# Probabilities copied by DMA and transposed as fp32r, and six held units for the mixing step

## The chip, the cores and the metric

The kernel runs on one core of one Trainium2 chip. The metric is the time of one execution on the device, in microseconds. A core has TensorE (PE, with its weight loads listed apart as PEld), VectorE (DVE), ScalarE (ACT), GpSimd (POOL) and SyncE (SP), which here only issues DMAs.

## The reference

Two layers: attention with a decay over 8 batches x 8 heads, 576 tokens, head size 64, and then a mixing layer over 512 channels.

```python
scores = q @ k.T / 8 + cum[:, None] - cum[None, :]   # cum = cumsum(log(clip(f)))
attn = softmax(where(causal, -1e9, scores))
x = concat_heads(attn @ v)                     # (8, 576, 512)
u = x + (x.transpose(0, 2, 1) @ U @ V).transpose(0, 2, 1)   # rank 32, over the tokens
out = u + maximum(u @ w_ch1, 0) @ w_ch2        # 512 -> 2048 -> 512
```

All of it is in fp32.

## The kernel before, in words

**Numbers in two parts.** Where precision is needed, an fp32 value is held as a high part rounded to fp32r and a low part, and a product is three fp32r matmuls (high by high, low by high, high by low). The first `NF = 6` pairs of heads use plain fp32 matmuls instead.

**Pairs and steps.** The attention works on pairs of heads: 4 pairs a batch, 32 in all (`p`). `step(t)` has ten slots (`s`), and handles three pairs at once: pair `p` is scored, the pair one step behind (`a`) has its probabilities transposed, and the one two steps behind (`c`) is multiplied with the values and normalised. For each of the two heads (`j`) and each of four blocks of 128 queries (`i`) `score` makes a tile of up to 512 columns; in slots 0 to 3 those of head 0, in slots 6 to 9 those of head 1 (two of them in 7 to 9 follow a first one at the end of 6). `score_tail` does the last 64 queries of both heads, in slots 4 and 5.

**What follows a score.** `defer(phase, fn, slots)` puts work off to a later slot, where it runs by phase. One slot after a score DVE adds the mask and takes the row extremum (L364), and ACT makes the exponential (L372, the tail at L400) into a tile of pool `sb2`, tag `P{i}`, or `Ptl`. In the next step `turn_p` transposes these tiles on PE, 128 x 128 at a time, against an identity (L444: 20 a pair), `turn_tail` the tail (L461: 4) and `turn_small` its last 64 columns (L479: 1). ACT copies each result from PSUM as the high part (L419), DVE subtracts for the low part (L422). `values` multiplies with the values (L568 to L574); for the result the halves of a PSUM tile are added crosswise, through a tile `cr` that ACT copies (L583) and DVE adds (L579). `turn_x` brings the result back, and it is scaled into `xn[b % 3]`.

**Mixing and feed-forward.** After the fourth pair of a batch follow ten mixing units, one a slot in the steps of `MIX`: five products with U and V (`hmix`, L656), four transposes of u (`tu`, L670) and that of the tail (`tv`, L679). Their PSUM tiles come from `psF`, which has two banks. The six of 16 blocks of the hidden layer that lie in the sweep are `ffn_units`: `l1` (L719, 12 matmuls a unit) and `l2` (L737, 6 matmuls a unit, three units to one `psF` tile). They fill PE between the attention's work (`run_filler`): by a credit in the slots of `ROOM`, and in the mixing step from the `HELD = 4` last units of the batch before, in slots 0, 1, 3 and 5. The sums of an `l2` tile and of x go through a tile `ost` to DRAM (`accd`), u goes to DRAM as `ud`; after the sweep the other ten blocks are computed from these.

**Order.** PE's order is the program's throughout, SP's too from step 8 on; a DMA issue that waits holds up all that follow on SP. The order on the other engines is set by the planner of the framework.

In the listing that follows the line numbers are those of the profile.

Of the kernel before, what the change touches and what calls it, by code (L numbers as in the profile page):

```python
# [18 lines left out]
DM = H * D  # L19
# [22 lines left out]
def tile_decay_attention_moe(ctx, tc, qk, v, f, U, V, w1, w2, out):  # L42
# [41 lines left out]
    sf2 = pool("sf2", 2)  # L84
# [6 lines left out]
    sb3 = pool("sb3", 3)  # L91
    psF = ctx.enter_context(tc.tile_pool(name="psF", bufs=2, space=PSUM))
# [28 lines left out]
    ident = cst.tile([P, P], F32, name="ident")  # L121
    make_identity(nc, ident)
# [16 lines left out]
    def decay_log():  # L139
        fr = sb.tile([B * H, S], F32, tag="xT", name="fr")  # L140
        fl = sb.tile([B * H, S], F32, tag="cr", name="fl")
        cm = sb.tile([B * H, 4, S], F32R, tag="PT", name="cm")
        return fr, fl, cm
# [46 lines left out]

    def load_w(u):
# [4 lines left out]
        if kind == "w2":  # L196

            spare = xn[NX - 1].rearrange("p c d -> p (c d)").bitcast(I32)
            if fc % 2:
                raw, a = spare[:, 1536:2560], sb.tile([P, 512], I32, tag="w2a", name=f"stg{u}")  # L200
            else:
                raw, a = spare[:, 0:1024], spare[:, 1024:1536]
# [142 lines left out]

    scored = [0]
# [8 lines left out]
    def score(p, j, i):  # L355
# [25 lines left out]
    def score_tail(p, x):  # L381
# [14 lines left out]
        def use():  # L396
            if x == 1:
                z["ptl"] = sb.tile([P, S], F32, tag="Ptl", name=f"Ptl{p}")
                for y in range(2):
                    nc.scalar.activation(  # L400
                        z["ptl"][:, hw * y : hw * y + hw], z["tl"][y][:, :hw], AF.Exp, bias=z["nm"][:, 9:10],
                        scale=-1.0, accum_out=z["sm"][:, 8 + y : 9 + y],
                    )

# [21 lines left out]
    def turn_p(p, j, g):  # L426
# [16 lines left out]
        for x, (c, i) in enumerate(grp):  # L443
            nc.tensor.transpose(tp[:, P * x : P * x + P], z["P"][j][i][:, P * c : P * c + P], ident)  # L444
# [12 lines left out]
    def turn_tail(p):  # L457
        z = st[p]
        tp = z["tv"][:, 512:1024]
        for c in range(NM):  # L460
            nc.tensor.transpose(tp[:, P * c : P * c + P], z["ptl"][:, P * c : P * c + P], ident)  # L461
# [13 lines left out]
    def turn_small(pa, px):  # L475

        tq = psT.tile([P, 512], F32, tag="T", name=f"Ty{pa}_{px}")
        if pa is not None:
            nc.tensor.transpose(tq[0:64, 0:P], st[pa]["ptl"][:, MAIN:S], ident)  # L479
# [75 lines left out]
    def values(p, j):  # L555
# [4 lines left out]
        if j == 0:  # L560
            z["xT"] = sb.tile([P, S], F32, tag="xT", name=f"xT{p}")
            z["cr"] = sb.tile([P, S], F32, tag="cr", name=f"cr{p}")
        VS, xT, cr = z["VS"], z["xT"], z["cr"]
# [13 lines left out]

        def total():
            nc.vector.tensor_tensor(xT[OWN[j]], pv[OWN[j], X0 : X0 + S], cr[OTH[j]], op=ALU.add)  # L579
# [3 lines left out]
        defer(1, lambda: nc.scalar.copy(cr[OTH[j]], pv[OTH[j], X0 : X0 + S]))  # L583
# [59 lines left out]
    def mix_units(b):  # L643
# [30 lines left out]
        def tv():  # L674
# [9 lines left out]
            def use():  # L684
                for x, t in enumerate((uh, ul)):
                    if b < B - 1:
                        nc.sync.dma_start(ud[b, :, x], t.bitcast(F32)[:, :, 0:MAIN])
                    if b % 2:
                        jt = b // 2
                        nc.sync.dma_start(ud[B, :, x, :, P * jt : P * jt + P], t.bitcast(F32)[:, :, MAIN : MAIN + P])  # L690

            defer(4, use, 2)
# [8 lines left out]
    def ffn_units(b):  # L701
# [3 lines left out]
        for t0, nt in groups:  # L705
# [24 lines left out]
            def l2(x, part, t0=t0, g=g):  # L730
# [14 lines left out]
                def use():  # L745
                    if b == B - 1 and ci < NM:
                        nc.vector.tensor_tensor(X[:, ci], ps, X[:, ci], op=ALU.add)
                        return
                    ost = sf2.tile([P, DM], F32, tag="ost", name=f"ost{b}_{ci}")
                    if ci < NM:  # L750
                        nc.vector.tensor_tensor(ost, ps, X[:, ci], op=ALU.add)  # L751
                        nc.sync.dma_start(accd[b, ci], ost)
                    else:
                        nc.vector.tensor_tensor(ost[0:64], ps[0:64], X[0:64, NM], op=ALU.add)
                        nc.vector.tensor_tensor(ost[64:128], ps[64:128], xn[(b - 1) % NX][0:64, NM], op=ALU.add)
                        nc.sync.dma_start(accd[B, b // 2], ost)

                defer(1, use)

# [9 lines left out]
    HELD = 4  # L769
# [485 lines left out]
```

## Time and profile before

| | |
|---|---|
| median of 3 runs | 1265.49 us (1256.07, 1265.49, 1266.22) |
| the profiled execution | 1256.17 us, its span 1254.3 us |
| PE busy | 1210.9 us, 97% of the span |
| PE weight loads | 1074.2 us, 86% |
| DVE, ACT, POOL busy | 893.8, 645.2, 325.2 us |
| DMA | 125.89 MB, mean 100 GB/s |

PE rows are matmuls, PEld rows weight loads. Matmuls are pipelined, so the sum of their durations is more than the time they take; the distance from one start to the next is what one of them costs. The attention sweep ends at about 700 us, the feed-forward work that was filled into it a little later, and what remains is the rest of the hidden layer.

### The profile page before, as it was taken

To read this page: it belongs to the slowest core of one execution; us is meant where nothing else is said; L and a number is where in the kernel's file an instruction comes from. 1 tells how busy PE (TensorE), PEld (TensorE's weight loads), DVE (VectorE), ACT (ScalarE), POOL (GpSimd) and SP (SyncE) were. 2 spreads that over 40 slices of the span, in tenths; PEclk is the share of its full clock that TensorE was granted. 3 is DMA by queue.
4 is the path that set the end of the run, shared out by engine and by line. 5 is a ranking of instruction groups with operands and counts; after the bars stand their busy time and mean duration, and the time that the engine had idled before them with its cause. 6 is when DMAs were issued, how large, how long until landed. Compare 5 with 4: busy or idle time off the path is not lost.

```text
span 1254.3 us, 21662 instructions
## 1 busy us (share of the span) xinstructions
PE 1210.9 (97%) x7686; PEld 1074.2 (86%) x7686; DVE 893.8 (71%) x2306; ACT 645.2 (51%) x1723; POOL 325.2 (26%) x310
## 2 busy tenths in 40 slices
PE   5999999999999999999999989999999999999998
PEld 3776888998898998988989878888988888888887
DVE  6767588778878768778777699976565565655553
ACT  5666787867777767768667343332122221212221
POOL 4353555434454443545442000000000000000000
PEclk9999999999999999999999999999999999999999
DMA  7435232532435325235413256121221303213010
GB/s 193 120 103 157 66 106 80 172 96 76 141 94 157 110 72 168 75 83 163 110 57 104 79 173 258 53 68 40 96 101 34 135 18 118 84 52 134 1 34 34
DMA packets 67547, 125.89 MB, mean 100 GB/s; under 512 B 7360, under 2 KB 31936, under 8 KB 65392
## 3 DMA queue, kind: packets, MB, share of 16 engines
q1 hardware_dynamic: 67312, 124.50, 32.3%
q8 instruction: 61, 1.00, 0.3%
q14 instruction: 46, 0.38, 0.1%
q10 hardware_dynamic: 128, 0.01, 0.0%
HBM read 88.68 MB, written 35.78 MB: 99 GB/s over the span
## 4 chain that ended last, share of the span: by engine, by line
PE 84%; DVE 9%; ACT 4%; issue 2%; DMA 1%; POOL 0%; SPq 0%; ACTq 0%; DVEq 0%; POOLq 0%
PE O L1004 20%; PE M L1097 16%; PE A L719 10%; PE B L737 9%; PE V L568 5%; PE T L444 4%; PE S L343 3%; PE S L340 2%; PE Hb L990 2%; PE S L344 2%; PE V L525 2%; PE Tt L628 1%; PE Tu L670 1%; PE St L340 1%; ACT G L303 1%
## 5 line engine op out<-in xcount | busy, mean ns | idle before, releaser
L1117 DVE TENSOR_TENSOR sum<-M,sum 128x256 f32<-128x256 f32 x280 | 114.6, 422 | 161.1 <-PE M L1097 159.8
L981 ACT ACTIVATE bh<-sum 128x256 fp32r<-128x256 f32 x160 | 66.7, 418 | 257.9 <-DVE sum L1117 257.9
L372 ACT ACTIVATE P<-S,nm 128x128 f32<-128x128 f32 (+3 forms) x256 | 136.2, 532 | 66.2 <-DVE nm L364 61.8
L364 DVE CUSTOM_DVE_ANT_0 S<-S,mask 128x128 f32<-128x128 f32 (+3 forms) x256 | 125.9, 495 | 59.9 <-PE S L344 39.0
L1004 PE MATMUL O<-b2h,bh 128*128 128x512 f32 x360 | 142.7, 396 | 0.0
L1004 PE MATMUL O<-b2l,bh 128*128 128x512 f32 x360 | 142.2, 395 | 0.0
L1004 PE MATMUL O<-b2h,bl 128*128 128x512 f32 x360 | 141.6, 393 | 0.0
L719 PE MATMUL A<-uh,w1h 128*128 128x256 f32 (+1 forms) x384 | 120.6, 314 | 1.7 <-DVE hl L723 1.7
L719 PE MATMUL A<-ul,w1h 128*128 128x256 f32 (+1 forms) x384 | 113.5, 296 | 0.0
L719 PE MATMUL A<-uh,w1l 128*128 128x256 f32 (+1 forms) x384 | 113.5, 295 | 0.0
L303 POOL CAST G<-qk 64x576 fp32r<-64x576 f32 x52 | 34.3, 661 | 255.5 <-PE St L344 150.7
L737 PE MATMUL B<-w2h,hh 128*128 128x512 f32 x216 | 90.2, 418 | 2.0 <-DVE ost L751 1.0
L444 PE MATMUL T<-ident,P 128*128 128x128 f32 x544 | 88.1, 279 | 0.3 <-DVE PT L422 0.3
L737 PE MATMUL B<-w2l,hh 128*128 128x512 f32 x216 | 85.0, 394 | 0.0
L737 PE MATMUL B<-w2h,hl 128*128 128x512 f32 x216 | 84.7, 392 | 0.0
L1004 PEld LDWEIGHTS O<-b2l,bh 128*128 128x128 f32 x360 | 67.6, 188 | 16.4
L422 DVE TENSOR_TENSOR PT<-T,PT 128x512 fp32r<-128x512 f32 (+1 forms) x156 | 79.0, 528 | 2.4 <-ACT PT L419 0.8
L568 PE MATMUL V<-PT,VS 128*128 128x448 f32 (+2 forms) x416 | 79.7, 334 | 0.0
L319 POOL TENSOR_TENSOR G<-qk,G 64x576 fp32r<-64x576 f32 x52 | 74.4, 1432 | 16.7 <-ACT G L303 15.5
L1004 PEld LDWEIGHTS O<-b2h,bl 128*128 128x128 f32 x360 | 67.9, 189 | 11.2
L343 PE MATMUL S<-G 128*128 128x128 f32 x208 | 71.9, 350 | 5.6 <-ACT P L372 2.9
L1004 PEld LDWEIGHTS O<-b2h,bh 128*128 128x128 f32 x360 | 67.9, 189 | 10.6
(224 smaller groups left out, 3423.9 us busy)
## 6 DMA issues: line engine op xcount, KB each, us to landing
qk<-in_qk_dram SPq DMA_DIRECT2D x104, 288.0 KB
u<-ud SPq DMA_DIRECT2D x16, 1024.0 KB
sr<-in_w_dram SPq DMA_DIRECT2D x20, 512.0 KB
vr<-in_v_dram SPq DMA_DIRECT2D x32, 256.0 KB
accd<-ost SPq DMA_DIRECT2D x32, 256.0 KB
xn<-accd SPq DMA_DIRECT2D x8, 1024.0 KB
out_dram<-xn SPq DMA_DIRECT2D x32, 256.0 KB
ud<-uh SPq DMA_DIRECT2D x7, 1024.0 KB
```

Source lines behind the costliest of these rows:

```text
L319: em.tensor_tensor(g[own, 1, cols], q[own], gf[own, 0, cols], op=ALU.subtract)
L343: nc.tensor.matmul(ps, G[j][:, 0, c0 : c0 + P], G[j][:, 2, cols], start=first, stop=False)
L364: nc.vector.tensor_tensor_reduce(ps[:, :w], ps[:, :w], mask[:, 512 - w : 512], scale=-SCALE, scalar=3.0e38, op0=ALU.add, op1=ALU.min, accu ...
L372: nc.scalar.activation(pt, ps[:, :w], AF.Exp, bias=z["nm"][:, col : col + 1], scale=-1.0, accum_out=z["sm"][:, col : col + 1])
L422: defer(2, lambda: nc.vector.tensor_tensor(dstl, src, dsth.bitcast(F32), op=ALU.subtract))
L444: nc.tensor.transpose(tp[:, P * x : P * x + P], z["P"][j][i][:, P * c : P * c + P], ident)
L568: nc.tensor.matmul(pv[:, X0 + lo : X0 + S], VS[:, c, j], pt[:, j, OC[c] + lo - P * c : OC[c] + S - P * c], start=x == 0 and c == 0, stop=F ...
L719: nc.tensor.matmul(ps[:, :nt], wt[:, fc, c], ut[:, c, sl], start=m == 0, stop=m == 3 * NDC - 1)
L737: nc.tensor.matmul(ps, ht[:, fc, P * x : P * x + P], wt[:, fc], start=fc == 0 and m == 0, stop=fc == NA - 1 and m == 2,)
L1004: nc.tensor.matmul(po, ht[:, P * x : P * x + P], wt_[i], start=k == 0 and m == 0, stop=k == NB - 1 and m == 2)
L1097: nc.tensor.matmul(ps, a[x][:, c], b[y][:, c], start=m == 0, stop=m == 5)
L1117: nc.vector.tensor_tensor(dst, ps, other, op=ALU.add)
```

## The change

Four things change.

- From pair six on (`p >= NF`) the exponential is written to a tile of a new pool `sb4` (four buffers, tag `stg`), and a DMA on SP's queue, one slot later, copies it to the tile `P{i}` or `Ptl`, which is now of type fp32r. The DMA sees both sides as fp32 and moves the bits as they are. The transposes of these tiles are made as fp32r, with an fp32r identity. The tile `cr` and one staging tile of the weights come from the same four buffers.
- The sums of the second layer are added into `xn` itself and stored from there two slots later; the two halves of the tails are stored one by one.
- The stores of u to DRAM go in pieces of 128 x 512, one a slot.
- `HELD` is 6 in place of 4, and in the mixing step units run in slots 0, 1, 3, 5, 7 and 8. The load of the decay rows of the next pair's head 0 is issued in slot 6 ahead of that slot's other work, in place of slot 7.

```diff
+    sb4 = pool("sb4", 4)
...
-    ident = cst.tile([P, P], F32, name="ident")
-    make_identity(nc, ident)
+    identr = cst.tile([P, P], F32R, name="ident")
+    ident = identr.bitcast(F32)
+    unit = sb.tile([P, P], F32, tag="xl", name="unit")
+    make_identity(nc, unit)
+    nc.gpsimd.tensor_copy(identr, unit)
...
+    def stage(name):
+        return sb4.tile([P, S], F32, tag="stg", name=name)
...
+    def turn(p, dst, src):
+        if p < NF:
+            nc.tensor.transpose(dst, src, ident)
+        else:
+            nc.tensor.transpose(dst.bitcast(F32R), src, identr)
...
-            pt = sb2.tile([P, w], F32, tag=f"P{i}", name=f"P{p}_{j}{i}")
+            pt = sb2.tile([P, w], F32 if p < NF else F32R, tag=f"P{i}", name=f"P{p}_{j}{i}")
             z["P"][j].append(pt)
+            e = pt if p < NF else stage(f"E{p}_{j}{i}")
             nc.scalar.activation(
-                pt, ps[:, :w], AF.Exp, bias=z["nm"][:, col : col + 1], scale=-1.0, accum_out=z["sm"][:, col : col + 1]
+                e[:, :w], ps[:, :w], AF.Exp, bias=z["nm"][:, col : col + 1], scale=-1.0,
+                accum_out=z["sm"][:, col : col + 1],
             )
+            if p >= NF:
+                defer(6, lambda: nc.sync.dma_start(pt.bitcast(F32), e[:, :w]))
...
+                if p >= NF:
+                    defer(6, lambda: nc.sync.dma_start(z["ptl"].bitcast(F32), e))
...
-            nc.tensor.transpose(tp[:, P * x : P * x + P], z["P"][j][i][:, P * c : P * c + P], ident)
+            turn(p, tp[:, P * x : P * x + P], z["P"][j][i][:, P * c : P * c + P])
...
+        def cross():
+            z["cr"] = stage(f"cr{p}_{j}")
+            nc.scalar.copy(z["cr"][OTH[j]], pv[OTH[j], X0 : X0 + S])
...
-                    if b < B - 1:
-                        nc.sync.dma_start(ud[b, :, x], t.bitcast(F32)[:, :, 0:MAIN])
+            pieces = [(x, c) for x in range(2) for c in range(NDC + 1) if (b < B - 1 if c < NDC else b % 2)]
+            for k, piece in enumerate(pieces):
+                defer(4, lambda piece=piece: store(*piece), 2 + k)
...
+                def store():
+                    if ci >= NM:
+                        for r, src in enumerate((X, xn[(b - 1) % NX])):
+                            nc.sync.dma_start(accd[B, b // 2, 64 * r : 64 * r + 64], src[0:64, NM])
+                    elif b < B - 1:
+                        nc.sync.dma_start(accd[b, ci], X[:, ci])
...
-    HELD = 4
+    HELD = 6
...
+            if s == 6 and NF <= nxt_p < NP:
+                place_decay(p + 1, 0)
...
-            if s == 7 and NF <= nxt_p < NP:
-                place_decay(p + 1, 0)
...
-                if filler and (s in (0, 1, 3, 5) or ending):
-                    run_filler()
+                for _ in range(1 if ending else {0:1,1:1,3:1,5:1,7:1,8:1}.get(s, 0)):
+                    if filler:
+                        run_filler()
```

More of the change, by code (lines that the diff above doesn't have):

```diff
@@ L140, in decay_log @@
         fr = sb.tile([B * H, S], F32, tag="xT", name="fr")
-        fl = sb.tile([B * H, S], F32, tag="cr", name="fl")
+        fl = sb.tile([B * H, S], F32, tag="Ptl", name="fl")
         cm = sb.tile([B * H, 4, S], F32R, tag="PT", name="cm")
@@ L199, in load_w @@
             if fc % 2:
-                raw, a = spare[:, 1536:2560], sb.tile([P, 512], I32, tag="w2a", name=f"stg{u}")
+                raw, a = spare[:, 1536:2560], stage(f"stg{u}").bitcast(I32)[:, 0:512]
             else:
@@ L460, in turn_tail @@
         for c in range(NM):
-            nc.tensor.transpose(tp[:, P * c : P * c + P], z["ptl"][:, P * c : P * c + P], ident)
+            turn(p, tp[:, P * c : P * c + P], z["ptl"][:, P * c : P * c + P])
         if p < NF:
@@ L478, in turn_small @@
         if pa is not None:
-            nc.tensor.transpose(tq[0:64, 0:P], st[pa]["ptl"][:, MAIN:S], ident)
+            turn(pa, tq[0:64, 0:P], st[pa]["ptl"][:, MAIN:S])
         if px is not None:
@@ L745, in use @@
                 def use():
-                    if b == B - 1 and ci < NM:
+                    if ci < NM:
                         nc.vector.tensor_tensor(X[:, ci], ps, X[:, ci], op=ALU.add)
                         return
[L749 to L756, printed above, removed]
+                    for r, src in enumerate((X, xn[(b - 1) % NX])):
+                        rows, own = slice(64 * r, 64 * r + 64), src[0:64, NM]
+                        nc.vector.tensor_tensor(own, ps[rows], own, op=ALU.add)
+                def store():
+                    if ci >= NM:
+                        for r, src in enumerate((X, xn[(b - 1) % NX])):
+                            nc.sync.dma_start(accd[B, b // 2, 64 * r : 64 * r + 64], src[0:64, NM])
+                    elif b < B - 1:
+                        nc.sync.dma_start(accd[b, ci], X[:, ci])
                 defer(1, use)
+                defer(6, store, 2)
             units += [(12 * max(nt / 2400, 0.107), lambda fc=fc, l1=l1: l1(fc)) for fc in range(NA)]
@@ L964, in tile_decay_attention_moe @@
     up = pool("up", 2)
+    up2 = pool("up2")
     hp_ = pool("hp", 4)
@@ L1031, in tile_decay_attention_moe @@
     Tl = sf.tile([P, 4, 2, HT], F32R, tag="ul", name="Tl")
-    tmp = [sf2.tile([P, 2, HT], F32, tag="ost", name=f"sum{x}") for x in range(2)]
+    tmp = [up2.tile([P, 2, HT], F32, name=f"sum{x}") for x in range(2)]
     tmp.append(sf.tile([P, 2, HT], F32, tag="TS", name="sum2"))
```

26 lines of the change are left out of this document (13 added, 13 removed).

## The prediction

> **What bounds the kernel now.** I read the first page for the balance of the engines, then the busy times of one window in the middle of the sweep, then the chain of waits in that window.
>
> ```profile
> span 1254.3 us, 21662 instructions
> PE 1210.9 (97%) x7686; PEld 1074.2 (86%) x7686; DVE 893.8 (71%) x2306; ACT 645.2 (51%) x1723; POOL 325.2 (26%) x310
> ...
> PEclk9999999999999999999999999999999999999999
> ...
> 200.00:700.00 500.00, 489.50 (x3329) 445.30 (x3328) 392.67 (x1107) 363.14 (x1019) 226.35 (x198) 1.00 0.39 111
> ...
> by line: PE A L719 20.2%; PE B L737 17.6%; PE V L568 11.1%; PE T L444 6.9%; PE S L343 5.7%; PE S L344 4.6%; issue 2.6%; PE Tt L628 2.4%; PE Tu L670 2.3%; PE St L343 1.9%; DVE PT L422 1.9%; PE St L344 1.8%; ACT G L303 1.7%; DVE ost L751 1.6%
> ```
>
> The window row gives, after its 500 us, the busy time of PE, weight loads, DVE, ACT and POOL, then the granted clock, the DMA share and GB/s. In the attention sweep PE is busy for 489.5 of 500 us at clock 1.00, DVE for 392.7 (79%), ACT for 363.1 (73%); the chain is almost all PE, and PE's transposes of the probabilities (L444) alone are 6.9% of it. So a microsecond taken off PE's stream in the sweep is a microsecond off the end, until DVE at 79% comes near. After the sweep the diff only moves buffers; I cost that stretch at nothing, since PE's stream there is the same.
>
> **Part 1, transposes as fp32r: the pace of one.** A matmul row shows its start and its duration, but matmuls are pipelined, so what counts is the distance between starts.
>
> ```profile
> 563.06 0.60 PE L461 MATMUL T_v<-ident,Ptl 128*128 128x128 f32 x4
> ...
> 570.41 0.22 PE L628 MATMUL Tt<-xh,Us 128*64 128x128 f32 x1
> 570.47 0.22 PE L628 MATMUL Tt<-xl,Us 128*64 128x128 f32 x1
> 570.53 0.22 PE L628 MATMUL Tt<-xh,Us 128*64 128x128 f32 x1
> ...
> 572.56 0.43 PE L679 MATMUL Tv<-ident,xn 64*128 64x64 f32 x4 [0.65 <-DVE ul L661]
> ...
> 92.16 2.34 PE L525 MATMUL V<-vr,PTh 128*128 128x64 f32 x20
> ...
> L461 PE MATMUL T_v<-ident,Ptl 128*128 128x128 f32 x128 | 19.7, 277 | 1.6 <-ACT PTh L419 1.6
> ```
>
> Four fp32 transposes fill 0.60 us; less one's own 277 ns, three steps take 0.323 us: 0.108 us a step. The stationary operand is the data, the moving one the identity's 128 columns. An fp32r matmul with 128 moving columns (L628) goes at 0.06 us a step. Is it the moving side that sets 0.108? The Tv row says so: there the weights also have 128 columns but only 64 columns move, and four fill 0.43 us. With a single one at 0.22 us (the L628 rows) that is 0.07 a step, so a transpose's weight load of 128 columns fits into 0.07. As fp32r I expect the step at the moving side's 0.06, a saving of 0.108 - 0.060 = 0.048 us each. The trace has no fp32r transpose, so this price has bounds: 0 if the load of fp32r weights goes slower than that of fp32 ones in a transpose, 0.048 if it doesn't. I take 0.048, because the Tv row is the only transpose with a short moving side, and it is a transpose.
>
> The rule that speaks against it is in the Trainium skill, TensorE: Matmul & The Clock Gate, section LDWEIGHTS: a weight load takes its columns divided by 1.2 GHz, whatever the contraction. An estimate from that page is 128 / 1.2 = 107 ns a transpose, and by it the change would save nothing. The L525 row agrees with the rule for ordinary fp32 matmuls, the Tv row disagrees for fp32 transposes; no run yet shows fp32r ones.
>
> **How many.** The page's groups count them for all 32 pairs.
>
> ```profile
> L444 PE MATMUL T<-ident,P 128*128 128x128 f32 x544 | 88.1, 279 | 0.3 <-DVE PT L422 0.3
> L444 PE MATMUL T_v<-ident,P 128*128 128x128 f32 x96 | 16.7, 284 | 0.2 <-DVE xT L581 0.2
> ...
> L479 PE MATMUL Ty<-ident,Ptl x25: 270/272/273, 173.4 to 693.4; 128*64 128x128 f32 x25
> ```
>
> (544 + 96) / 32 = 20 main transposes a pair, 128 / 32 = 4 of the tail, 1 small one: 25 a pair. Pairs 6 to 31 are 26, so 650 transposes: 650 x 0.048 = 31.2 us off PE's stream. The last row also gives the pace of the sweep: 24 steps in 520 us, 21.7 us a pair, 2.17 a slot. Transposes of xT and xn stay fp32.
>
> **Part 2, the copies by DMA.** Nine SBUF copies a pair (eight probability tiles, one tail) now stand between the exponential and the transpose, on SP's queue.
>
> ```profile
> 0.74 0.60 SPq L772 DMA_DIRECT2D fr<-in_f_dram  x1
> ...
> 3.55 0.45 DVE L777 TENSOR_SCALAR fr<-fr 64x576 f32<-64x576 f32 x1 [1.24 <-DMA fr<-in_f_dram]
> ...
> L752 SPq DMA_DIRECT2D accd<-ost x28: 326/332/351, 156.8 to 723.6; - x28
> L324 SPq DMA_DIRECT2D G<-cumd x52: 641/662/740, 71.4 to 663.0; - x52
> ...
> q1 hardware_dynamic: 67312, 124.50, 32.3%
> ...
> qk<-in_qk_dram SPq DMA_DIRECT2D x104, 288.0 KB
> ...
> SPq L288 <- POOL VS L178: 35.5, 12, 4.8
> ```
>
> *Latency.* The trace has no SBUF-to-SBUF copy; the nearest is the load of fr, whose reader starts 3.55 - 0.74 = 2.8 us after its issue. The latest copy that a transpose needs is that of the fourth tile of a head: score in slot 3, exponential in 4, copy in 5, transpose in slot 0 of the next step. That is five slots, 10.8 us, against 2.8 plus at most a pair of qk loads ahead of it. At 111 GB/s for a share of 0.39 the engines move 285 GB/s, so 2 x 288 KB cost 2.1 us: 4.9 us. Hidden.
>
> *SP's time.* Nine issues at 0.33 (L752) to 0.66 (L324) are 3.0 to 5.9 us of 21.7; hidden by SP's own waiting. *Bandwidth.* A pair copies 128 x (2 x 1280 + 576) x 4 bytes = 1.6 MB; 26 make 41.7 MB, at 32.3% per 124.5 MB another 10.8% of the span: the window's share goes from 0.39 to about 0.6. Hidden.
>
> *Stage buffers.* The exponentials and the two cross halves take turns in four buffers, 11 uses in 10 slots; the shortest turn gives a copy two slots, 4.3 us, before ACT may write there again. Against 2.8 that holds; against 4.9 behind qk loads ACT waits 0.6 us, and ACT has 27% to spare. I take 0 and keep the other end for a rival. What is queued behind such a wait on ACT: the evacuations of the transposes and DVE's subtractions after them. Behind SP's new waits for exponentials: the qk and v loads, the decay rows, the accd and ud stores, whose readers come slots or batches later; the decay rows move from slot 7 to ahead of slot 6's copies, where the tail's scores of slot 5 that they wait for are just done.
>
> **Part 3, six held units and the mixing step.** PE's stalls that recur are in the mixing step, once a batch, six times after pair six:
>
> ```profile
> 556.29 0.50 PE L737 MATMUL B<-w2h,hh 128*128 128x512 f32 x1 [0.17 <-DVE ost L751]
> ...
> 563.54 0.66 PE L670 MATMUL Tu<-ident,xn 128*128 128x128 f32 x4
> ...
> 566.36 0.66 PE L670 MATMUL Tu<-ident,xn 128*128 128x128 f32 x4 [0.35 <-DVE ost L751]
> 569.12 0.65 PE L670 MATMUL Tu<-ident,xn 128*128 128x128 f32 x4
> ...
> 571.73 0.69 DVE L661 TENSOR_TENSOR ul<-Tu,uh 128x512 fp32r<-128x512 f32 x1
> ```
>
> With the 0.65 before Tv that is 1.17 us a mixing step, 7 us in six. Two more units of six matmuls now run in slots 7 and 8. They move work, they add none; at best they cover all 7 us. At worst they cost: a unit block holds one of the two psF banks from its first third to its last, now in slots 5 to 8, so Tu1 to Tu3 share the other bank, and each waits for the evacuation of the one ahead. That took 572.42 - 569.12 = 3.3 us, against distances of 2.8 us (563.54 to 566.36 to 569.12): 0.5 a time, two times, 6 us in six steps. Between -7 and +6 I take 0. In these steps the shorter transposes also leave waits that do not shrink: I give up half of 6 x 25 x 0.048 = 7.2, so 3.6 us.
>
> **Part 4, the rest.** Results added into xn and stored from there: the same DVE operations, without a buffer; the stores add issues on SP, 4 for the tails (two for one in four batches) and 42 for the transposed sums (eight for two in seven batches), 46 x 0.33 = 15 us of SP's time over the whole sweep, hidden. The identity's copy adds one POOL operation at the start, where POOL is done before PE's first matmul:
>
> ```profile
> 6.14 1.33 POOL L117 TENSOR_SCALAR_AFFINE_SELECT mask<-mask 64x64 f32<-64x64 f32 x2
> ...
> 12.26 4.61 PE L340 MATMUL S<-qk 68*128 68x128 f32 x8 [12.26 <-DMA qk<-cm]
> ```
>
> It has 12.26 - 7.47 = 4.8 us of cover. Nothing for all of these.
>
> **Sum.** -31.2 + 3.6 = -27.6 us. The profiled execution took 1256.2 us (span 1254.3 and 1.9 around it), which gives 1228.6. The runs shown are 1256.1, 1265.5 and 1266.2: with the profiled one, two executions at 1256 and two at 1266. The sum is for the lower level, the upper would add about 9.7; I name a time between, 1228.6 + 4 = 1233.
>
> **Rivals.** *Weights bound (0.2).* In a transpose the fp32r weights load at the 0.109 a step of the L525 row ((2.34 - 0.27) / 19) instead of Tv's 0.07. Then 650 x 0 is saved and the copies buy nothing: 1256, at the upper level 1266. For it: fp32r is loaded like fp32 in ordinary matmuls; against it: the Tv row. It is what the skill's LDWEIGHTS rule, above, would make of the change.
>
> *Half (0.2).* The step comes out midway, 0.084, or DVE takes over: at 393 us of work in 500 - 650 x 0.048 x 500 / 564 (26 pairs at 21.7) = 472 it is 83% busy, and waits for its evacuations may eat half. 1242.
>
> *Slower (0.13).* Stage buffers come free too late. SP waits in order; its v load waited for POOL 12 times, up to 4.8 us, and the copy of slot 5 stands behind it. 4.8 + 2.8 + 2.1 = 9.7 us against the three slots (6.5 us) until that buffer is written again makes ACT 3.2 us late, and with two score banks PE then stands. From 27.6 / 26 = 1.1 us a pair on it eats the whole gain; at 2 us a pair the time is 1228.6 + 52 = 1281. Against it: only 12 of the waits, and ACT's slack.
>
> **How the numbers follow.** Forecast 0.47 (1233, its own range 1219 to 1246: 1228.6 less 7 and some error below, plus 6 and the upper level above), half 0.2, weights bound 0.2, slower 0.13. About 1% is what a measurement can tell from no change. Faster by over 1%: the forecast and most of half, 0.63; same: weights bound and the rest of half, 0.25; slower 0.12. The range takes in half whole and most of weights bound: 1216 to 1262.
>
> **What would show it.** Right: fp32r transposes at 0.06 a step; about 20.6 us from one small transpose to the next; DMA share near 0.6; ACT's idle time before exponentials not ended by DMA. Weights bound: steps still at 0.108. Slower: exponentials that wait for a DMA of the stage tiles, and score matmuls that wait for ACT. Part 3: the stalls before Tu and Tv, summed per mixing step, against 1.17 us.

## The result, and the profile after

The changed kernel is slower by 0.7%: the ratio of its time to that of the kernel before is 1.0073, with an interval of 1.0051 to 1.0094 (medians 1267.0 and 1255.3 us, 20 executions each). That is 6 to 12 us more, where I had forecast 23 less.

In some executions the granted PE clock falls for a while in the first 140 us, which costs up to some 10 us; the medians, ratios and intervals include such executions. The stretch of twenty pairs that is read below lies behind that fall: its granted clock is 1.00 in the trace of every run.

First the page of the changed kernel: span, busy times, SP's queue, and the chain of waits by engine; then that chain in the kernel before.

```profile
span 1265.7 us, 22409 instructions
...
PE 1207.3 (95%) x7686; PEld 1065.8 (84%) x7686; DVE 899.9 (71%) x2306; ACT 646.3 (51%) x1723; POOL 326.6 (26%) x311
...
q1 hardware_dynamic: 101744, 166.26, 42.5%
...
PE 75%; DVE 13%; ACT 6%; DMA 3%; issue 2%; POOL 1%; SPq 0%; ACTq 0%; POOLq 0%; DVEq 0%
```

```profile
PE 84%; DVE 9%; ACT 4%; issue 2%; DMA 1%; POOL 0%; SPq 0%; ACTq 0%; DVEq 0%; POOLq 0%
```

PE has 3.6 us less to do by its busy time, but the span is 11.4 us longer. In the window of the sweep that the prediction read (columns as there), and in the chain of waits of that window:

```profile
200.00:700.00 500.00, 481.13 (x3322) 434.81 (x3323) 399.72 (x1110) 365.21 (x1024) 228.40 (x199) 1.00 0.61 183
```

```profile
by line: PE A L743 19.5%; PE B L761 15.3%; PE V L586 6.9%; PE S L349 4.8%; PE S L350 3.8%; issue 3.4%; PE T L356 3.3%; DVE S L376 2.9%; DVE sm L432 2.2%; ACT E L385 2.1%; ACT Et L417 2.1%; PE St L349 2.0%; PE T_v L356 2.0%; PE St L350 2.0%;
```

PE is busy for 481.1 us of the 500 in place of 489.5: the shorter work has become idle time. The transposes T have fallen from 6.9% to 3.3% of the chain, and what has come into it are DVE and ACT, among them a line that was not in the chain before at all: `sm` at L432, an operation on 128 x 9 numbers, with 2.2% of 500 us, 11 us. DMA's share is the 0.6 that was forecast.

The pace of the sweep is read from the small transpose that each pair has once. These are the third and the twenty-third of the 25 that the prediction's row counts, those of pairs 9 and 29, five whole batches apart (some expectations below call them marks 9 and 29); first the kernel before, then the changed one:

```profile
213.30 0.27 PE L479 MATMUL Ty<-ident,Ptl 128*64 128x128 f32 x1
...
653.14 0.27 PE L479 MATMUL Ty<-ident,Ptl 128*64 128x128 f32 x1
```

```profile
216.59 0.22 PE L356 MATMUL Ty<-ident,Ptl 128*64 128x128 f32 x1
...
655.95 0.22 PE L356 MATMUL Ty<-ident,Ptl 128*64 128x128 f32 x1
```

Twenty pairs took 439.8 us and now take 439.4. I call this distance "20 pairs" in all that follows. Runs that differ only outside this stretch agree in it within 0.1 us (435.8 and 435.8 for e4 and e7 below), so it tells tenths apart where the whole time can't. One more small transpose follows the 25, of a result alone, at 709.84 us before and 715.45 us after. From it to the end of the span it was 544.5 us and is 550.2.

So what makes the changed kernel's trace 11.4 us longer lies outside the 20 pairs: 3.3 us ahead of them, 2.8 in the three pairs behind them, and 5.8 in the rest. The 3.3 us ahead go with two short falls of the clock, whose mean from 140 to 200 us is 0.94 in this trace and 1.00 in that of before. Two questions follow: why 20 pairs gained nothing, and what the parts cost behind them.

### The profile page after: what moved, and what is told of

It is laid out like the page before. It is cut to its first block, busy times and chain, and to the rows that moved or that the text cites. A ratio compares the mean times of both kernels' runs of the same rounds, so it can differ in the third digit from the quotient of the medians.

```text
span 1265.7 us, 22409 instructions
## 1 busy us (share of the span) xinstructions
PE 1207.3 (95%) x7686; PEld 1065.8 (84%) x7686; DVE 899.9 (71%) x2306; ACT 646.3 (51%) x1723; POOL 326.6 (26%) x311
## 4 chain that ended last, share of the span: by engine, by line
PE 75%; DVE 13%; ACT 6%; DMA 3%; issue 2%; POOL 1%; SPq 0%; ACTq 0%; POOLq 0%; DVEq 0%
PE O L1033 20%; PE M L1126 15%; PE A L743 9%; PE B L761 7%; PE V L586 3%; PE S L346 3%; PE S L349 2%; PE Hb L1019 2%; PE V L544 2%; PE S L350 2%; PE T L356 2%; DVE S L376 1%; PE St L346 1%; DMA sr<-in_w_dram 1%; ACT E L385 1%
## 5 line engine op out<-in xcount | busy, mean ns | idle before, releaser
L385 ACT ACTIVATE E<-S,nm 128x128 f32<-128x128 f32 x208 | 110.1, 530 | 50.5 <-DVE nm L376 37.3
L743 PEld LDWEIGHTS A<-uh,w1h 128*128 128x128 f32 x384 | 73.0, 190 | 6.7 <-DVE hl L747 3.6
```

What stands on the lines that cost most here:

```text
L385: nc.scalar.activation(e[:, :w], ps[:, :w], AF.Exp, bias=z["nm"][:, col : col + 1], scale=-1.0, accum_out=z["sm"][:, col : col + 1],)
L743: nc.tensor.matmul(ps[:, :nt], wt[:, fc, c], ut[:, c, sl], start=m == 0, stop=m == 3 * NDC - 1)
```

## The experiments

All against the kernel before on the same chip. "End" is the time from that last small transpose, of a result alone, to the end of the span. The last column says how much full clock is missing in that end.

| run | what it is | ratio, interval | 20 pairs | end | clock missing |
|---|---|---|---|---|---|
| | before | 1 | 439.8 | 544.5 | 0 |
| | after | 1.0073 [1.0051, 1.0094] | 439.4 | 550.2 | 1.7 |
| e1 | after, four held units | 1.0032 [1.0013, 1.0051] | 439.0 | 546.8 | 0 |
| e2 | after, no copies | 1.0045 [1.0013, 1.0076] | 435.8 | 549.6 | 3.4 |
| e3 | after, fp32 transposes | 1.0048 [1.0015, 1.0081] | 440.6 | 548.4 | 1.7 |
| e4 | before, six held units | 0.9994 [0.9963, 1.0025] | 435.8 | 548.2 | 3.4 |
| e5 | after, fp32 transposes, no copies | 1.0031 [0.9995, 1.0066] | 437.4 | 547.7 | 0 |
| e6 | after, `hmix` addition first | 1.0058 [1.0024, 1.0091] | 438.5 | 548.2 | 0 |
| e7 | e4, four held units at the end | 0.9958 [0.9926, 0.9990] | 435.8 | 546.7 | 1.7 |
| e8 | e2, `hmix` first, four held units at the end | 0.9999 [0.9969, 1.0029] | 435.9 | 546.6 | 0 |
| e9 | after, row sums off DVE | 1.0052 [1.0027, 1.0078] | 432.6 | 551.4 | 3.4 |
| e10 | e7, row sums off DVE | 0.9965 [0.9941, 0.9990] | 430.8 | 547.4 | 1.7 |
| e11 | e2, four held units at the end, row sums off DVE | 0.9963 [0.9933, 0.9993] | 427.5 | 546.8 | 0 |
| e12 | e11 with the copies | 1.0046 [1.0019, 1.0073] | 431.3 | 549.2 | 0 |
| e13 | e11, copies that nobody reads | 1.0027 [0.9987, 1.0066] | 434.1 | 546.7 | 0 |
| e14 | e12, copies on ACT's queue (five executions) | 1.0160 [1.0110, 1.0210] | 449.6 | 546.8 | 0 |
| e15 | e11, a matmul for each group of transposes | 0.9914 [0.9884, 0.9945] | 418.5 | 546.9 | 0 |
| e16 | e12, no copy of the tail | 0.9979 [0.9944, 1.0014] | 428.2 | 547.6 | 0 |
| e17 | e10, fp32r transposes, no copies | 0.9950 [0.9919, 0.9981] | 427.5 | 543.7 | 0 |
| e18 | before, row sums off DVE | 1.0013 [0.9982, 1.0043] | 436.4 | 544.4 | 0 |

The clock in the end, with the kernel before first and then e4 (the columns are those of the window row above, the clock third from the right):

```profile
700.00:740.00 40.00, 35.85 (x240) 31.49 (x239) 32.71 (x68) 16.31 (x35) 0.00 (x0) 1.00 0.37 127
```

```profile
700.00:740.00 40.00, 36.00 (x208) 30.57 (x207) 31.83 (x65) 15.17 (x30) 0.00 (x0) 0.91 0.36 119
```

A mean of 0.91 over 40 us means that some 3.4 us of full clock are missing; over 705 to 720 us alone it is 0.77. PE is busy for most of such a stretch, so as an estimate the end is longer by about as much. Less this, the ends fall into two groups: 543.7 to 545.7 us with the stores and buffers of before (before, e4, e7, e10, e17, e18), 546.2 to 549.2 with the new ones.

### The parts one by one: e1 to e5

e1, `HELD` back to 4:

```diff
-    HELD = 6
+    HELD = 4
-    {0:1,1:1,3:1,5:1,7:1,8:1}
+    {0:1,1:1,3:1,5:1}
```

> The changed kernel with HELD at 4 again and units in slots 0, 1, 3 and 5 of the mixing step. Theory A (the held units cost): after the last pair's small transpose the changed kernel loses 5.8 us more against the kernel before (566.4 to 560.6 us from there to the end), and its six mixing steps are 0.5 us longer than two more units explain; so this run takes about 8 to 9 us less than the changed kernel, 1258. Theory B (the copies cost): the two units only move work, this run stays at 1265 to 1268.

e2, no copies, ACT writes the exponentials into the fp32r tiles (so the probabilities are rounded to fp32r):

```diff
-            e = pt if p < NF else stage(f"E{p}_{j}{i}")
+            e = pt
-            if p >= NF:
-                defer(6, lambda: nc.sync.dma_start(pt.bitcast(F32), e[:, :w]))
```

> The changed kernel without the copies: ACT writes the exponentials into the fp32r tiles itself, which rounds the probabilities to fp32r, and the nine DMAs a pair are gone. Six held units stay. Theory B (the copies cost, through late data and stage buffers): 10 us or more come back, 1257 or less. Theory A: the copies are hidden, this run stays within 3 us of the changed kernel, 1264 to 1268.

e3, the copies stay, the tiles and transposes are fp32:

```diff
-            pt = sb2.tile([P, w], F32 if p < NF else F32R, ...)
+            pt = sb2.tile([P, w], F32, ...)
-            nc.tensor.transpose(dst.bitcast(F32R), src, identr)
+            nc.tensor.transpose(dst, src, ident)
```

> The changed kernel with its copies, but the probabilities are transposed as fp32 again. From the traces a transpose takes 94 ns as fp32r and 111 as fp32 with what it costs its neighbours, so 650 x 17 ns = 11 us are to be lost if PE still sets the time: 1278. If the changed kernel waits for ACT and DMA anyway (theory B), less than 4 us are lost: 1267 to 1271.

e4, the kernel before with `HELD = 6` and the units in slots 0, 1, 3, 5, 7 and 8:

> The kernel before with nothing changed but HELD at 6 and units in slots 0, 1, 3, 5, 7 and 8 of the mixing step. Theory A: it takes 8 us more than the kernel before, 1263. Theory B: within 2 us of it, 1253 to 1257.

e5, both edits of e2 and e3, which leaves the held units, the buffers and the new stores:

> The changed kernel without copies and with the probabilities transposed as fp32: what is left of the change are the six held units and the new stores. From the ninth to the twenty-ninth small transpose (twenty pairs) the copies with fp32 transposes took 440.6 us, the kernel before with six held units 435.8. If the copies are what costs there, this run takes 435 to 436.5 us for the twenty pairs and 1255 to 1257 in all; if the stores in pieces cost, it keeps 440 us and about 1262.

By the 20 pairs the four parts are: held units 435.8 - 439.8 = -4.1 (e4 against before), new stores 437.4 - 435.8 = +1.7 (e5 against e4), fp32r 435.8 - 437.4 = -1.6 (e2 against e5), copies 439.4 - 435.8 = +3.5 (after against e2; e3 against e5 says +3.1). Together -0.5. Each is a few us, and the part that was to bring 31 us, 24 of them in 20 pairs, brings 1.6.

Behind the 20 pairs, the held units lose 2.9 us of what they won: e4's last three pairs take 59.6 us in place of 56.7. Its end is 3.7 us longer too, but by that estimate 3.4 of it are the missing clock. Its ratio, 0.9994, shows neither gain nor loss. The new stores and buffers make the end 2.9 us longer (547.7 in e5 against 544.8, which is e4's less the missing clock). The ratios go the same way, 1.0031 for e5, 1.0045 for e2 and 1.0073 for all, but their intervals overlap, and that of e5 takes in 1.

Two expectations fell here. Theory A of e1 named the right time (1258.6 us came out) for a cost of the held units that e4 doesn't have, and e3, back to fp32 transposes, was to be slower than the change and at 1.0048 is not.

**The pace of an fp32r transpose.** The same place of the sweep in e10 (fp32) and in e11 (fp32r), PE's timeline: a score, three transposes, and the first two matmuls of a unit; for e11 also two groups of four transposes.

```profile
444.95 0.28 PE L344 MATMUL S<-G 128*128 128x256 f32 x1
445.06 0.49 PE L443 MATMUL T<-ident,P 128*128 128x128 f32 x3
445.31 0.42 PE L718 MATMUL A<-uh,w1h 128*128 128x384 f32 x1
445.57 0.33 PE L718 MATMUL A<-uh,w1l 128*128 128x384 f32 x1
```

```profile
440.61 0.53 PE L356 MATMUL T<-ident,P 128*128 128x128 f32 x4
...
441.16 0.28 PE L350 MATMUL S<-G 128*128 128x256 f32 x1
441.28 0.37 PE L356 MATMUL T<-ident,P 128*128 128x128 f32 x3
441.48 0.41 PE L738 MATMUL A<-uh,w1h 128*128 128x384 f32 x1
441.73 0.34 PE L738 MATMUL A<-uh,w1l 128*128 128x384 f32 x1
...
452.72 0.46 PE L356 MATMUL T_v<-ident,Ptl 128*128 128x128 f32 x4
```

The prediction read a step as the group's time, less one's own (0.25 here), by the steps in the group. For the three transposes this gives (0.37 - 0.25) / 2 = 0.06 us, as forecast; for the tail's four it is 0.07, and for the other four 0.09. But it counts only the steps inside a group. From the start of the three to the next matmul it is 0.25 us in fp32 and 0.20 in fp32r: the two steps are 0.1 us shorter together, and the next matmul starts 0.08 us behind the last transpose in place of 0.03.

From the start of the transposes to the second matmul behind them it is 0.51 us in fp32 and 0.45 in fp32r: 0.06 for three, 0.020 each. Now take all groups of three and four beside which PE doesn't wait, from the start of the matmul ahead to the start of the second one behind, less those two's own columns (0.23 us for 512). By the middle value a transpose costs 0.111 us in the kernel before and 0.094 in the changed one. So it saves 0.017, 11 us for 650 of them and 8.5 in 20 pairs, a third of what I had put down.

### The mixing step: e6 to e8

Of those 8.5 us only 1.6 were seen. The mixing steps showed where some of it went: 20.3 us before, 23.1 with six held units and fp32 transposes (e4), but 23.7 with fp32r (e2), though fp32r should make them shorter (one of the five in 20 pairs, the second, is 1.4 us shorter wherever six units are held). From e4 to e2 the five mixing steps together are 3.1 us longer, and the other fifteen steps 3.1 us shorter. My first theory was the order of two operations on DVE. e6 puts the addition of `hmix` first; e7 and e8 also try a cure for the longer end:

```diff
-                defer(4, lambda: nc.vector.tensor_tensor(X[0:kk, i], ps[0:kk], ...))
+                defer(0, lambda: nc.vector.tensor_tensor(X[0:kk, i], ps[0:kk], ...))
```

```diff
-            elif len(filler) > HELD and s in ROOM:
+            elif len(filler) > (held := HELD if t <= MIX[B - 2] else 4) and s in ROOM:
```

> The changed kernel, but DVE's addition of a product with U and V is put off with phase 0 in place of 4, so that the planner puts the fifth one ahead of a result of the small transpose, and the mask of a score ahead of a subtraction, as in the kernel before. Theory: the shorter transposes changed DVE's order, and that is why a mixing step takes 23.7 us with fp32r transposes and 23.1 with fp32 ones, with copies or without. Then the mixing step falls to 23.1 to 23.3 and the run to 1262 to 1264. Rival: PE waits for banks that the two more units hold, whatever DVE's order: 23.7 and 1266 to 1268.

> The kernel before with six held units up to the mixing step of the seventh batch and four after it. Holding six gained 3.9 us up to the last small transpose and lost 3.7 us behind it, where the units kept back are missing between the last ranks and products. If that is so, only the gain is left: 1250 to 1252. If the loss at the end has another cause, 1254 to 1256.

> All three together: no copies (ACT rounds the probabilities to fp32r), six held units up to the seventh mixing step and four after it, and the addition with phase 0. If the three causes add up, 10 us for the copies, 4 for the end and 4 for DVE's order come off the changed kernel's 1267: 1249 to 1251, just below the kernel before, with all that fp32r transposes give. If PE still set the pace by itself, 650 x 17 ns more would show against the same kernel with fp32 transposes, 1240 to 1243.

The mixing step stayed at 23.7 us in e6 and e8: that theory fell, and e8 took 1256.4 us in place of 1249 to 1251. The cure for the end isn't shown either: e7's end is 1.5 us shorter than e4's, but it has 1.7 us less of missing clock, and its last three pairs take 59.5 us as e4's do. e7's ratio, 0.9958, is below 1, but its interval overlaps with e4's.

The timeline of the mixing step of e2 has the reason, DVE and POOL beside PE:

```profile
584.36 1.44 POOL L324 TENSOR_TENSOR G<-qk,G 64x576 fp32r<-64x576 f32 x1
...
584.42 1.40 DVE L428 TENSOR_SCALAR sm<-sm 128x9 f32<-128x9 f32 x1 [0.38 <-ACT P L385]
...
588.05 0.43 PE L356 MATMUL T_v<-ident,P 128*128 128x128 f32 x3 [0.66 <-DVE xT L599]
```

And the same place in e5:

```profile
573.62 0.17 DVE L425 TENSOR_SCALAR sm<-sm 128x9 f32<-128x9 f32 x1 [0.37 <-ACT P L382]
...
573.62 1.45 POOL L324 TENSOR_TENSOR G<-qk,G 64x576 fp32r<-64x576 f32 x1
...
573.82 0.22 DVE L426 RECIPROCAL rv<-sm 128x9 f32<-128x9 f32 x1
```

At 573.62 the small operation starts together with POOL's subtraction and takes 0.17 us (at 316.69 in the same trace the two also start within 0.01 us, and there it takes 1.45). At 584.42 it starts 0.06 us behind and takes 1.40: it ends when POOL ends (585.80 and 585.82). DVE is then 1.2 us late, and PE waits 0.66 us for `xT`. The reciprocal at 573.82 lies wholly beside the same subtraction and takes its 0.22. The Trainium skill says this in SBUF — State Buffer, section "SBUF: two separate sides": DVE and GpSimd share one pair of ports as an exclusive lock for the whole instruction, and a DVE operation takes part in it when it has two SBUF inputs or runs in a two-port mode. These traces agree with it: the `sm` operations wait, the reciprocal does not.

What the lock costs can be read from e5 by itself. In two of its five mixing steps the second operation is held, for 1.45 us at 316.69 and for 1.19 us here:

```profile
400.35 1.43 POOL L324 TENSOR_TENSOR G<-qk,G 64x576 fp32r<-64x576 f32 x1
400.62 1.19 DVE L425 TENSOR_SCALAR sm<-sm 128x9 f32<-128x9 f32 x1 [0.66 <-ACT P L382]
```

These two steps are 0.8 us longer each than the same ones of e4 (22.5 and 23.9 in place of 21.7 and 23.1), and the other three are as there (23.1). That is the whole of e5's +1.7, which I had put down to the new stores. The stores may still have moved the operation by the few tenths of a us that decide whether it meets POOL. With fp32r, in e2 and in the changed kernel, the second operation is held in all five mixing steps, in e4 in none.

That the lock meets another operation after the change stands in the groups of operations, first of the kernel before, then of the changed one: mean ns behind the comma.

```profile
L412 DVE TENSOR_TENSOR sm<-sm 128x1 f32<-128x1 f32 x32 | 23.6, 738 | 4.3 <-ACT Ptl L400 4.3
...
L413 DVE TENSOR_SCALAR sm<-sm 128x9 f32<-128x9 f32 x32 | 8.7, 273 | 6.3 <-ACT P L372 6.3
```

```profile
L432 DVE TENSOR_SCALAR sm<-sm 128x9 f32<-128x9 f32 x32 | 17.7, 552 | 12.4 <-ACT E L385 10.4 <-ACT P L385 1.9
...
L431 DVE TENSOR_TENSOR sm<-sm 128x1 f32<-128x1 f32 x32 | 17.4, 545 | 7.9 <-ACT Et L417 5.8 <-ACT Ptl L417 2.1
```

Before, it was the first of the two that stood behind POOL: from pair six on L412 took over 0.4 us in 23 of 26 pairs, the second, L413, in none. After, the first (L431) does so in 13 pairs, and the second (L432), the one right ahead of the work that PE waits for, in 11. Each of these ends within 0.04 us of the end of a POOL operation. In all, the two took 32.3 us before and take 35.1.

### Taking the lock away: e9 to e12 and e18

One edit takes both operations off DVE. The sum of the tail's two columns goes to ACT, and the addition of 1e-9 is left out:

```diff
-        nc.vector.tensor_tensor(sm[:, 8:9], sm[:, 8:9], sm[:, 9:10], op=ALU.add)
-        nc.vector.tensor_scalar(sm[:, 0:9], sm[:, 0:9], 1e-9, None, op0=ALU.add)
+        nc.scalar.activation(sm[:, 8:9], sm[:, 8:9], AF.Identity, bias=sm[:, 9:10])
         nc.vector.reciprocal(z["rv"][:, 0:9], sm[:, 0:9])
```

> The changed kernel with one edit: of the three small DVE operations that turn a pair's row sums into reciprocals, the first (sum of the two tail columns) goes to ACT and the second (adding 1e-9, left out here) is dropped; only the reciprocal stays on DVE. Theory (DVE's small operations on SBUF stand behind a POOL subtraction of 1.44 us, and PE then waits for DVE): DVE loses about 1.1 us a pair, the mixing step falls from 23.74 to 23.1 us or below, 20 pairs from mark 9 to 29 from 439.4 to 434 or less, the time to about 1260. Rival (PE's waits come from something else): the mixing step stays at 23.7, 20 pairs at 439, the time at 1264 to 1267. A third outcome, the reciprocal itself taking 1.4 us in place of the others, would show in its mean above 0.22 us and leave most of the time as it is.

> The kernel before with six held units (four after the seventh mixing step) and the row sums' edit: fp32 transposes, no copies. Theory: with fp32 transposes the DVE operations were mostly not in PE's way, so little is gained: 20 pairs from 435.8 to 434 to 436, the time 1251 to 1253, mixing step 23.1. Rival (DVE is what paces the pairs): 1.1 us less of DVE work a pair shows here too, 20 pairs at 430 or below, the time at 1247 or below.

> The changed kernel without copies (ACT writes the exponentials rounded into the fp32r tiles), with four held units after the seventh mixing step and the row sums' edit. It differs from the one with fp32 transposes and the same edits by the transposes' type and by the new stores. Theory (the transposes' gain was hidden behind DVE and POOL): 20 pairs fall from 435.9 to 428 to 432, so 4 to 8 us below the fp32 one, and the time to 1246 to 1250. Rival (other waits hold the pair): 20 pairs stay at 434 to 436 and the time at 1252 to 1256, the same as the fp32 one within 2 us.

> The changed kernel with its copies, four held units after the seventh mixing step and the row sums' edit: the copies' price with DVE relieved, against the same without copies. Theory: copies cost what they cost before, 3 to 4 us in 20 pairs, so about 3 to 5 us of the time; 1250 to 1255 in all. Rival (copies cost nothing once DVE has room): within 1 us of the one without copies.

> The kernel before with the row sums' edit alone. If the small DVE operations behind POOL are in its way as they were with six held units (5.1 us in 20 pairs): 20 pairs from 439.8 to 434 to 436, time 1249 to 1252. If they only came into the way by the six held units: 438.5 to 440, time 1254 to 1256.

What is left on DVE in e9, by its group, is never held up:

```profile
L432 DVE RECIPROCAL rv<-sm 128x9 f32<-128x9 f32 x32 | 6.8, 213 | 13.8 <-ACT E L385 12.3 <-ACT P L385 1.4
```

The edit is worth 439.4 - 432.6 = 6.7 us in 20 pairs of the changed kernel (e9), 435.8 - 427.5 = 8.3 without copies (e2 to e11), 5.1 with fp32 transposes and six held units (e7 to e10), and 3.4 in the kernel before (e18). It takes away the two operations and not only their waiting: unhindered they take 0.15 and 0.17 us, 6.4 us in 20 pairs, so outside the mixing steps the lock's share isn't shown. In the five mixing steps their own time is 1.6 us, and e9 is 7.0 us shorter there and e11 7.2, which is nearly all that it is worth in these two. So the lock cost most with fp32r: with it fp32r was worth 1.6 in 20 pairs (e5 to e2, or nothing, e4 to e2), without it 430.8 - 427.5 = 3.3 (e10 to e17, below, which differ in the transposes alone). The mixing step, 0.6 us longer with fp32r before, is now 0.25 shorter (22.21 in e11, 22.46 in e10). The rival of e10, that DVE's time counts with fp32 transposes too, came nearer than my theory there, and for e11 the theory's 4 to 8 us were too much.

The whole time followed only in part: e12 was to take 1250 to 1255 us and took 1260.9, and e18 has 3.4 us less in 20 pairs and no gain in its ratio. The edit costs 1.2 us at the start (two of the first steps take 16.3 and 13.3 us in place of 15.5 and 13.0), and what else it loses outside the 20 pairs, where the granted clock differs from one execution to the next, was not settled.

### Where the rest of the saving is: e15

> The kernel without copies, with four held units at the end and the row sums' edit; from pair seven on each group of three or four transposes is replaced by one fp32r matmul over as many columns (its values are not the transposed probabilities: this part of the computation is left out). By the transposes' 0.094 us and 0.4525 ns a column a group of four goes from 376 to 232 ns, one of three from 282 to 174: 0.86 us of PE work a pair, 17.3 us in 20 pairs. If PE still bounds the pairs with fp32r: 20 pairs fall from 427.5 to 410 to 413. If other waits hold them by now (which would explain 3.3 in place of 8 us): less than half of it, 419 to 427.

```diff
+            e = z["P"][j][3]
+            nc.tensor.matmul(tp[:, 0 : P * len(grp)], e[:, 0:P], e[:, 0 : P * len(grp)], start=True, stop=True)
```

PE's work in 20 pairs falls by a worked-out 17.3 us, the time by 427.5 - 418.5 = 9.0: half, between the two expectations. PE is no longer the only bound. The waits of PE and of its weight loads between 220 and 640 us (in all, times, longest) show what takes its place: first e10, then e11, then e15.

```profile
PEld S L343 <- ACT Ptl L400: 3.3, 12, 0.7
...
PE S L343 <- ACT Ptl L400: 0.4, 1, 0.4
```

```profile
PEld S L349 <- ACT Ptl L415: 5.8, 12, 1.1
...
PE S L349 <- ACT Ptl L415: 3.0, 6, 0.7
...
PEld B L756 <- DVE xn L674: 2.9, 4, 0.7
```

```profile
PEld S L349 <- ACT Ptl L415: 7.8, 12, 1.3
...
PE S L349 <- ACT Ptl L415: 4.3, 6, 0.9
PEld B L764 <- DVE xn L682: 4.0, 5, 0.8
```

The less PE has to do, the longer its scores wait for ACT to empty a bank with the tail's exponentials, and its units for DVE. These two waits are seen to grow; that they make up all of the difference was not shown (a PEld row and a PE row can be of the same wait, so they don't add up).

### The copies: e13, e14 and e16

The waits of the changed kernel, same window, and one of them in the chain:

```profile
PEld S L349 <- ACT E L385: 4.2, 10, 1.3
...
ACT E L385 <- DMA Ptl<-Et: 3.5, 6, 1.5
...
PE S L349 <- ACT E L385: 2.4, 7, 1.1
...
ACT E L385 <- DMA P<-E: 1.9, 1, 1.9
```

```profile
511.58 5.04 DMA Ptl<-Et
...
516.73 0.09 ACT E L385
```

An exponential waits for a copy out of the stage buffer that it is to overwrite. That copy, of the tail, took 5.04 us from issue to landing behind two qk loads and a store of u; PE's next scores wait for the exponential. The step that holds it took 19.0 us, and without copies (e2) it takes 17.1: 1.9 of the 3.5 us. Three runs on it. e13 keeps the transfers, but out of the finished tiles into two spare ones that nobody reads (its stage pool has two buffers, for `cr` alone); e14 issues the copies on ACT's queue; e16 lets ACT write the tail's exponentials straight into the fp32r tile:

```diff
-                defer(6, lambda: nc.sync.dma_start(pt.bitcast(F32), e[:, :w]))
+                defer(6, lambda: nc.sync.dma_start(sink(w), pt.bitcast(F32)))      # e13
+                defer(6, lambda: nc.scalar.dma_start(pt.bitcast(F32), e[:, :w]))   # e14
```

```diff
-                e = z["ptl"] if p < NF else stage(f"Et{p}")
+                e = z["ptl"]
-                if p >= NF:
-                    defer(6, lambda: nc.sync.dma_start(z["ptl"].bitcast(F32), e))
```

> ACT writes the exponentials rounded into the fp32r tiles, as in the kernel without copies, and the DMAs still run at the same place with the same sizes, but out of these tiles into a tile that nobody reads; four held units at the end and the row sums' edit as before. Theory A (the copies cost by waits: stage buffers that come free late, transposes that find their data late): the load alone costs at most 1 us, 20 pairs at 427.5 to 428.5, time 1250 to 1253. Theory B (they cost by load, on SP's queue or on the 16 DMA engines, so that other transfers come later): 20 pairs at 430 to 431.5, time 1257 to 1261.

> The changed kernel with four held units at the end and the row sums' edit, and its copies issued on ACT's queue in place of SP's, so that they stand behind no load or store that waits. If SP's order makes them late: 20 pairs fall from 431.3 to 428 to 429.5, ACT's exponentials no longer end idle time that a stage copy released, time 1252 to 1256. If the latency of a copy or the load on the DMA engines is what costs: 431 or more, and ACT pays its own issues besides, time 1260 or more.

> The changed kernel with four held units at the end and the row sums' edit, its eight probability tiles copied as there, but the tail's exponentials written straight into the fp32r tile: 8 copies a pair and 10 uses of the four stage buffers in place of 9 and 11. If waits for the tail's copy and its buffer are what costs: 20 pairs fall from 431.3 to 428 to 429. If the cost goes by the bytes, the tail has 18% of them: 430.5.

e16 answers it: without the tail's copy 3.1 of the 3.8 us that the copies cost in 20 pairs are gone (431.3 to 428.2, against 427.5 with none), where its share of the bytes would be 0.7. The same waits in e12 and in e16:

```profile
ACT E L385 <- DMA Ptl<-Et: 5.4, 6, 1.8
...
PEld S L349 <- ACT E L385: 4.2, 11, 1.3
```

```profile
ACT E L385 <- DMA P<-E: 3.6, 2, 1.8
...
PEld S L349 <- ACT E L385: 1.5, 7, 0.3
```

ACT still waits for copies of the eight tiles, but the wait of PE behind it falls from 4.2 to 1.5 us. So eight copies of a pair are nearly hidden, and the ninth with its turn of the buffers is not; which of the two, its latency or its buffer, was not separated. e14 tells nothing on SP's order, since an issue on ACT costs ACT too much:

```profile
L390 ACTq DMA_DIRECT2D P<-E x208: 472/472/1126, 131.8 to 707.0; - x104
```

Nine of 0.47 us are 4.2 us of ACT's time a pair, and 20 pairs took 18.4 us more than with SP's queue. e13 is not clean either: its two spare tiles held up SP's queue, and with it the loads. The SP queue's and POOL's waits there, 220 to 640 us:

```profile
SPq L396 <- DMA sink<-P: 48.8, 22, 3.5
SPq L396 <- DMA sink<-Ptl: 47.6, 20, 4.3
```

```profile
POOL G L315 <- DMA qk<-in_qk_dram: 24.1, 6, 5.4
```

Its 20 pairs are 6.6 us longer than e11's though nobody waits for a copy's data, which points to the late qk loads; it does not show that the changed kernel's copies make them so late. A ring of more than four stage buffers was not tried.

### The stores: e17

The kernel before with e10's edits and fp32r transposes of tiles that ACT writes rounded; its own stores and buffers:

> The kernel before (its stores, its cross tile, its sums through an own buffer) with six held units (four after the seventh mixing step), the row sums' edit, and fp32r transposes of tiles into which ACT writes rounded exponentials; no copies. It differs from the fp32 one with the same edits by the transposes alone. If the new stores cost the 1.6 us in 20 pairs that fp32 runs showed: 20 pairs at 425.5 to 426.5 against 427.5 with them, and the time at 1246 to 1251. If they cost nothing here: 427.5 and 1250 to 1252.

Twenty pairs took 427.5 us as in e11, so the new stores cost nothing there, as the lock in two mixing steps of e5 also says. The end is 3.1 us shorter (543.7 and 546.8, both at full clock). e5 against e4 has 2.9 and e1 against the kernel before 2.4, so the new stores or buffers cost 2 to 3 us after the last pair. What in them does that was not traced. With 0.9950 (1247.0 us) e17 has the lowest ratio of the kernels that transpose all probabilities, 2 to 10 us below the kernel before, but the intervals of e7, e10 and e11 overlap with its own; as in e2, its probabilities are rounded, which the change with its copies avoids.

## Why the prediction was wrong, point by point

**What bounds the kernel.** "A microsecond taken off PE's stream in the sweep is a microsecond off the end, until DVE at 79% comes near" was the step that failed most. The whole-window shares, DVE 79% and ACT 73%, hid that at certain places of each pair one of them is just in time. Of 8.5 us less PE work in 20 pairs fp32r gave nothing with the lock in place (e4 and e2, both 435.8), 3.3 without, and e15 gave half of its 17.3. What holds the other 5 us is not shown beyond the two waits of e15.

**Part 1, the pace.** Mis-sized: the saving of 0.048 a transpose, 31.2 us in all, measured 0.017 to 0.020 with the neighbours, 11 us. "The step at the moving side's 0.06" did come out, but only in groups of three; in groups of four it was 0.07 and 0.09. Two mistakes are in it. The row L628, from which I took 0.06, has 64 columns of weights (128*64), half of a transpose's, and the only bound that I had for 128, Tv's 0.07, was above it. And a step read inside a group leaves out the matmul behind the group, which starts 0.05 us later behind fp32r transposes than behind fp32 ones; the distance from the neighbour ahead to the second one behind holds it. The rule of the Trainium skill (TensorE: Matmul & The Clock Gate, section LDWEIGHTS), 107 ns for 128 columns, was too high for fp32r (0.094 with the neighbours). Its estimate of no saving came nearer to 0.017 than my 0.048. The rival "half" named 0.084 and 1242: its saving, 0.024, was the nearest, its time was wrong.

**How many.** 25 transposes a pair and 650 in all held.

**Part 2, the copies.** "Hidden" was right for the latency that the transposes see (none waits for a copy's data in the rows above), for the DMA share (0.61 for "about 0.6") and nearly for eight of the nine copies. It was wrong for the stage buffers: I had the right number, 4.9 us behind qk loads against a shortest turn of 4.3, and took 0 for it because ACT had 27% to spare. The chain shows 5.04, and the copies cost 3.1 to 3.8 us in 20 pairs, 3.1 of them by the ninth (e16). The rival "slower" had this mechanism at 13%, at a bigger price.

**Part 3, the held units.** Zero in sum was right by the ratio (e4: 0.9994), and for another reason than the one given: two more units made the mixing step 23.1 - 20.3 = 2.8 us longer, which is two units of six matmuls at 0.23 us, so they covered no stall there; 20 pairs still gained 4.1, and the last three pairs lost 2.9. The 3.6 us put down for mixing steps had the right sign and another cause: with fp32r they became longer by 0.6 us each, by the lock.

**Part 4, the rest.** "Nothing for all of these" was right in 20 pairs (e17 and e11 agree) and wrong behind the last pair, by 2.4 to 3.1 us (e1, e5, e17).

**What would show it.** Of the marks I had named, the step of 0.06 came out in groups of three, and the DMA share did; but a pair took 22.0 us, not 20.6, and exponentials did wait for DMA. None of the cases held whole: a smaller saving, a lock that moved and swallowed it, and two small costs taken as nothing.

## What to carry to other kernels

Before counting a saving on the busiest engine, look up which other engine ends each recurring place of a step, not its share of the window, and measure a short instruction from neighbour to neighbour rather than inside its group. Small DVE operations like the two here, which stand near GpSimd operations on SBUF, are to be counted with GpSimd's duration, not their own, until a trace shows that they aren't held; taking two of them away was worth more here than the faster transposes. For a staging buffer between an engine and a DMA, compare the copy's whole latency, behind the loads queued ahead of it, with the buffer's shortest turn (5.04 against 4.3 us here), whatever the writer has to spare on average. And before the end of a run is put down to the program, read the granted clock there.

## What the runs showed of the hardware

A 128 x 9 scalar addition on DVE that takes 0.17 us by itself took 1.40 us when it started 0.06 us behind a GpSimd subtraction of 1.44 us (e2), and 1.45 at most (e5); a 128 x 1 addition took 0.74 in the mean of the kernel before. A 128 x 9 reciprocal beside the same subtraction took its 0.22 us. Three or four fp32r transposes of 128 x 128 cost 0.094 us each with their neighbours against 0.111 in fp32. A DMA issue on ACT's queue took 0.47 us of ACT's time. In e18's trace the granted PE clock was 0.61 from 80 to 100 us and 0.72 from 100 to 140, with a mean of 0.985 over the whole execution, where another execution of the same kernel had a mean of 0.999; e4's fell to 0.77 from 705 to 720 us.
